# A fused top-k attention and gated feed-forward kernel: the second product's place in the order of TensorE

## The chip, the cores and the metric

The kernel runs on one core of a Trainium2 chip. A core has five engines that run their own queues in order and wait for each other by semaphores: TensorE (PE; its weight loads are shown apart as PEld), VectorE (DVE), ScalarE (ACT), GpSimd (POOL) and SyncE (SP, which here only issues DMAs). The metric is the time of one execution on the device in microseconds, given as the median over runs. Lower is better.

## The reference

Eight batches of eight heads, 576 tokens, head dimension 64. Each row of scores keeps its 32 largest entries, the rest is masked, and softmax and the product with V follow. The heads are then laid side by side, and a feed-forward part with a cosine gate is applied to the 4608 tokens. All in float32.

```python
scores = scale * np.matmul(q, k.transpose(0, 1, 3, 2))
kth = np.partition(scores, -top_k, axis=-1)[..., -top_k:-top_k + 1]
scores = np.where(scores >= kth, scores, -1000000000.0)
attn = softmax(scores)                       # sum in the denominator + 1e-09
x = np.matmul(attn, v)  ->  (B*S, H*D) = (4608, 512)
h = x @ w_in                                 # 512 x 2048
g = h * np.cos(h)
out = g @ w_out                              # 2048 x 512
```

## The kernel before, in words

**Units and slots.** The work of attention is cut into 144 units: 36 blocks of 128 tokens, each with four pairs of heads. A main loop has one slot a unit. In slot i, VectorE searches the 32 largest scores of unit i (four rounds of L359 and L364 on `rest`, then on `low`). Meanwhile ScalarE masks and exponentiates unit i-1 (L378, L387) and copies the scores of unit i+1 out of PSUM (`take_scores`, L253 and L257). GpSimd prepares unit i-2 for its transposition by DMA (`split`, L410 for the probabilities and L412 for the reciprocals `rden`), and it computes the lower halves of unit i's folded scores (L283, L292).

**TensorE's order** is written out by the emission of a slot, since each engine runs its instructions in the order in which they are emitted. A slot has three places where pieces of the feed-forward part are fed to TensorE. Feed A comes first. Then come the scores (L242) of the next units, two units in every even slot, and in slots with remainder 2 mod 4 the product P@V (`values`, L475) of the last block's four units. Feed B comes after the last round of the search has been emitted, and feed C closes the slot. So one block corresponds to four slots with remainders 0 to 3, and P@V of one block stands in each slot of remainder 2. After it VectorE multiplies with the reciprocals and writes the block's `xT` (`take_values`, L491 and L499), between the last two searches of that slot.

**The feed-forward part.** A block has eight items of the first product (`ff1`, L553). Each item computes two of the 16 column tiles of `h`, and the profile shows it as 16 matmul rows of 128 columns. Two items fill one PSUM bank. ScalarE empties a bank with two instructions (`take_first`, L567 and L569), into the scaled `g` and the rounded `x`. Two banks make one g tile of 1024 columns, so a block has two g tiles. A g tile then goes through GpSimd (`reduce_first`, L589; `reduce_second`, L598), ScalarE (`sines`, L608, in odd slots) and GpSimd again (`gate`, L615, which multiplies by the cosine). The block has also eight items of the second product (`ff2`, L628), two f each (f = 0, 2, ... 14), which read the gated g as weights and accumulate in one bank `o`; each is shown as four rows of 512 columns. Items f = 0 to 6 read the first g tile, f = 8 to 14 the second. ScalarE empties `o` (`take_second`, L638) and issues the DMA of the output. First and second product share two PSUM banks (tag `mm`).

**The planner.** `plan[i % 4]` lists for each feed of a slot what is tried there: 0 stands for an item of the first product, 1 for one of the second. An item is issued only if `can_first` or `can_second` allows it; otherwise it is passed over. `ff["tick"]` counts feeds, `ff["now"]` counts slots from 1. `can_second` asks that the slot count has reached a start value, that the w_out rows are decoded, and that the g tile in question was gated at least `lag` ticks ago. Gating is emitted in a slot just before feed B (`gate(1)`), and notes the tick of that slot's feed A. Sines are emitted in odd slots only, so a g tile is gated in an odd slot. `take_banks` empties full banks at several places of a slot. After the 144 slots a tail (`drain`, `forward`) works off what is left.

**The first slots.** The weights come as 64-bit words and are decoded in the first dozen slots by ScalarE, VectorE (L151) and GpSimd (L160). In slots 8 to 10 the fold is done by VectorE alone (`fold_now`, L275).

Of the kernel before, what the change touches and what calls it, by code (L numbers as in the profile page):

```python
# [30 lines left out]
def kernel(  # L31
# [16 lines left out]
    NP = H // 2  # L48
# [47 lines left out]
    ff = {"live": 0, "tick": 0, "now": 0, "end": False, "kind": 0, "half": 0, "open": 0, "late": False}  # L96
# [81 lines left out]
    NU = len(units)  # L178
# [333 lines left out]
    for w in widths:  # L512
# [10 lines left out]
    second = deque(  # L523
        (blk, i, f) for blk in blocks for i in range(blk["w"] // P) for f in range(0, NF, 2)
    )
# [125 lines left out]
        return ff["now"] > NP + 2 and (i % 4 > 0 or ff["live"] + staged() < CHUNKS)  # L651

    def can_second():
        if not second or ff["now"] < 2 * NP + 3:
            return False
        blk, i, f = second[0]

        lag = 3 if ff["now"] < NU - NP else 2
        gated = sum(ff["tick"] >= t + lag for t in blk["gated"])
        return gated * 1024 // blk["w"] >= f + 2 and wq["ready"] >= NC * NF // FC + f + 2  # L660

    def item(kind):
        if not (can_first, can_second)[kind]():
            return False
        if kind == 0:
            ff1(*first.popleft())
        else:
            ff2(*second.popleft())
        return True
# [68 lines left out]
    def send(x):  # L738
# [6 lines left out]

    plan = (
        ((0, 0), (1,), (1,)),
        ((0, 0), (1, 1), (0,)),
        ((0,), (1,), ()),
        ((1, 0, 0), (1, 1), ()),  # L750
    )

# [148 lines left out]
```

## Time and profile before

| | us |
|---|---|
| median of 3 runs | 1412.53 |
| lowest and highest | 1411.86, 1413.45 |
| span of the profiled execution, first to last instruction | 1410.6 |
| TensorE matmul rows busy | 1354.6 (96%) |
| VectorE busy | 1336.9 (95%) |
| ScalarE busy | 1140.9 (81%) |
| GpSimd busy | 1165.3 (83%) |

The profile is of one execution; it gives its span, and no time of its own beside it. A row of the order of time reads: start in us from the span's start, duration in us, engine, line, operation, output and inputs by tile name, shapes, and the number of instructions merged into the row; in brackets the idle time of the engine before it and what ended it. In the windows view the columns are the stretch, its length, the busy time of each engine with the number of instructions, the granted share of TensorE's clock, the DMA share and GB/s. Matmul rows overlap their successors a little, since their ends are modelled; the time that a piece takes is read from start to start.

The granted clock of TensorE is 0.975 as a mean over the span, and 1.00 in every stretch of 40 us between 120 and 1400 us. The first 120 us are different from the rest: TensorE is busy there for 68.3 of 120 us, and VectorE for 110.6.

### The profile page before, as it was taken

The page shows a single profiled execution, that of the slowest core. Times are in us where ns is not written, and L with a number is a line of the kernel's source. Part 1 is how long each engine was busy: PE and PEld are TensorE (multiplying, and loading weights), DVE is VectorE, ACT ScalarE, POOL GpSimd, SP SyncE. Part 2 cuts the span into 40 slices and gives each one's busy share as a digit, 9 for nine tenths or more (in the row PEclk, how much of TensorE's full clock was granted, in tenths as well). Part 3 has the DMA queues.
Part 4 walks back from the last instruction along what each step waited for, and adds up shares of the span by engine and source line. Part 5 has one row for each costly group of instructions (what it writes and reads, how often), then busy time and mean ns, then how long its engine had stood idle before and what let it go on. Part 6 is the DMA issues. An engine that isn't in the chain of part 4 may idle for free.

```text
span 1410.6 us, 32284 instructions
## 1 busy us (share of the span) xinstructions
PE 1354.6 (96%) x11264; PEld 977.2 (69%) x11264; DVE 1336.9 (95%) x5004; ACT 1140.9 (81%) x2043; POOL 1165.3 (83%) x804
## 2 busy tenths in 40 slices
PE   5558999999999999999999999999999999999998
PEld 3445777777777777777777777777777777777775
DVE  7999999999999999999999999999999999999931
ACT  7887888888888888888888888888888888888831
POOL 4778988888888888888888888888888888898810
PEclk6788999999999999999999999999999999999999
DMA  9566776867675576668666576666766566655540
GB/s 291 193 196 181 204 178 169 203 172 196 162 177 152 161 199 159 181 160 197 174 170 159 152 181 187 170 170 160 207 165 165 158 174 166 148 157 146 152 101 15
DMA packets 427442, 240.12 MB, mean 170 GB/s; under 512 B 375952, under 2 KB 392592, under 8 KB 427280
## 3 DMA queue, kind: packets, MB, share of 16 engines
q1 hardware_dynamic: 420720, 224.22, 61.3%
q10 hardware_dynamic: 6560, 13.85, 2.8%
q8 instruction: 88, 1.44, 0.4%
q14 instruction: 74, 0.61, 0.1%
HBM read 45.09 MB, written 101.19 MB: 104 GB/s over the span
## 4 chain that ended last, share of the span: by engine, by line
PE 91%; DVE 7%; ACT 1%; DMA 0%; POOL 0%; issue 0%; SPq 0%; POOLq 0%
PE o L628 36%; PE mm L553 35%; PE rim L475 10%; PE sc L242 8%; DVE top L359 3%; PE rim L242 2%; DVE rest L364 2%; DVE low L364 1%; DVE rest L267 1%; DVE w_out L151 0%; DVE w_in L151 0%; DMA st<-in_moe_w_in_dram 0%; PE warm L844 0%; DVE low L275 0%; ACT s L387 0%; ACT s L378 0%
## 5 line engine op out<-in xcount | busy, mean ns | idle before, releaser
L553 PEld LDWEIGHTS mm<-xT,w_in 128*128 128x128 f32 x4608 | 537.9, 192 | 70.4 <-issue 65.5
L553 PE MATMUL mm<-xT,w_in 128*128 128x128 f32 x4608 | 539.2, 275 | 2.4 <-DVE xT L491 1.7
L628 PE MATMUL o<-w_out,g 128*128 128x512 f32 x1152 | 524.7, 599 | 0.0
L359 DVE MAX8 top<-rest 128x8 f32<-128x288 f32 x1152 | 479.0, 451 | 0.0
L364 DVE MATCH_REPLACE8 rest<-top,rest 128x288 f32<-128x288 f32 x864 | 376.7, 444 | 0.0
L628 PEld LDWEIGHTS o<-w_out,g 128*128 128x128 f32 x1152 | 207.7, 190 | 219.5 <-issue 214.8
L410 POOL COPY halves<-s 128x2304 uint16<-128x2304 uint16 x140 | 294.9, 2107 | 43.3 <-ACT s L387 40.1
L378 ACT ACTIVATE s<-s,top 128x576 f32<-128x576 f32 x288 | 207.6, 768 | 111.1 <-DVE top L352 99.0
L359 DVE MAX8 top<-low 128x8 f32<-128x288 f32 x576 | 241.8, 449 | 0.4 <-POOL low L292 0.4
L387 ACT ACTIVATE s<-s,nd 128x576 f32<-128x576 f32 x288 | 220.4, 769 | 1.1
L292 POOL TENSOR_TENSOR low<-low,rest 128x576 int32<-128x576 int32 x141 | 199.3, 1413 | 11.0
L283 POOL TENSOR_TENSOR low<-s 128x576 int32<-128x576 int32 x141 | 199.6, 1415 | 6.4 <-ACT s L259 6.4
L598 POOL TENSOR_TENSOR x<-g,x 128x1024 f32<-128x1024 f32 x68 | 161.2, 2370 | 5.7
L242 PE MATMUL sc<-k,q 64*64 64x448 f32 (+1 forms) x1120 | 145.6, 564 | 16.2 <-DVE low L275 9.8
L615 POOL TENSOR_TENSOR g<-g,x 128x1024 f32<-128x1024 f32 x68 | 161.0, 2367 | 0.0
L257 ACT COPY s<-rim 64x256 f32<-64x256 f32 (+1 forms) x280 | 103.1, 368 | 61.6 <-PE rim L475 60.0
L475 PE MATMUL rim<-ring,v 128*64 128x128 f32 (+1 forms) x2560 | 139.0, 268 | 0.0
L475 PEld LDWEIGHTS rim<-ring,v 128*64 128x64 f32 x2560 | 130.0, 139 | 6.5 <-issue 5.7
L253 ACT COPY s<-sc 128x896 f32<-128x896 f32 (+1 forms) x144 | 128.4, 892 | 3.3 <-PE sc L242 3.2
L567 ACT ACTIVATE g<-mm 128x512 f32<-128x512 f32 x144 | 85.2, 592 | 56.5 <-PE mm L553 55.5
L364 DVE MATCH_REPLACE8 low<-top,low 128x288 f32<-128x288 f32 x288 | 125.4, 443 | 0.0
L267 DVE TENSOR_TENSOR rest<-sc,s 128x576 f32<-128x576 f32 x144 | 107.7, 748 | 7.1 <-ACT s L259 6.6
(55 smaller groups left out, 1155.7 us busy)
## 6 DMA issues: line engine op xcount, KB each, us to landing
rows<-halves SPq DMA_DIRECT2D x140, 640.0 KB, 3.5
out_dram<-ob ACTq DMA_DIRECT2D x36, 256.0 KB, 2.1
q<-in_q_dram SPq DMA_DIRECT2D x31, 288.0 KB, 4.4
st<-in_moe_w_in_dram SPq DMA_DIRECT2D x16, 512.0 KB, 5.8
v<-in_v_dram SPq DMA_DIRECT2D x32, 256.0 KB, 4.2
k<-in_k_dram SPq DMA_DIRECT2D x31, 144.0 KB, 4.2
k<-in_k_dram SPq DMA_DIRECT2D x32, 128.0 KB, 4.5
st<-in_moe_w_out_dram SPq DMA_DIRECT2D x8, 512.0 KB, 5.1
```

The costliest lines, as they stand in the source:

```text
L242: nc.tensor.matmul(to[r0 : r0 + rows, rim_bank(r0, j) if k0 else place(u["hp"], j), 0 : k1 - k0], st["q"][d, q0 : q0 + rows], st["k"][d, k ...
L283: nc.gpsimd.tensor_tensor(out=u["low"].bitcast(I32), in0=s[:, :, 0:HS], in1=s[:, :, HS:S], op=ALU.add)
L292: nc.gpsimd.tensor_tensor(out=low, in0=low, in1=u["rest"][:, :, HS:S].bitcast(I32), op=ALU.subtract)
L359: nc.vector.max(to[:, j], src[:, j])
L364: nc.vector.match_replace(rest[:, j], to[:, j], src[:, j], NEG)
L378: nc.scalar.activation(out=s[:, j], in_=s[:, j], func=AF.Prelu, bias=less[:, j], scale=1.0, alpha=FAR)
L387: nc.scalar.activation(out=s[:, j], in_=s[:, j], func=AF.Exp, bias=nd[:, j : j + 1], scale=SCALE, accum_out=den[:, j, 0:1],)
L410: nc.gpsimd.tensor_copy(out=halves[:, :, 0 : 2 * S], in_=s.rearrange("p (k h) -> p h k", h=2))
L475: nc.tensor.matmul(to[d, r], lhsT, rhs, start=(bank, j) not in begun, stop=c == NT - 1 and u in us[-2:] and r0 + rows == P,)
L553: nc.tensor.matmul(mm[:, at : at + w], w_in[f // FC][:, c, (f % FC) * P : (f % FC + 1) * P], blk["xT"][:, c], start=c == 0, stop=c == NC - 1,)
L598: nc.gpsimd.tensor_tensor(out=x, in0=g, in1=x, op=ALU.subtract)
L628: nc.tensor.matmul(o, g[:, at : at + P], w_out[f], start=f == 0, stop=f == NF - 1)
```

## The change

Two places of the planner are edited. The table for slots with remainder 1 and 2 gets another order: in remainder 1, feed B tries two items of the first product in place of two of the second, and feed C one of the second in place of one of the first; in remainder 2, feed A tries one of the second in place of one of the first. In `can_second`, the start value goes from 2*NP + 3 (11) to 2*NP + 2 (10), that is, from slot 10 to slot 9, and the lag from three ticks to one, except for the last four slots and the tail, where it stays at two. Nothing else is edited: all tiles, all instructions and their shapes are as before.

```diff
     def can_second():
-        if not second or ff["now"] < 2 * NP + 3:
+        if not second or ff["now"] < 2 * NP + 2:
             return False
         blk, i, f = second[0]
 
-        lag = 3 if ff["now"] < NU - NP else 2
+        lag = 1 if ff["now"] < NU - NP else 2
         gated = sum(ff["tick"] >= t + lag for t in blk["gated"])
...
     plan = (
         ((0, 0), (1,), (1,)),
-        ((0, 0), (1, 1), (0,)),
-        ((0,), (1,), ()),
+        ((0, 0), (0, 0), (1,)),
+        ((1,), (1,), ()),
         ((1, 0, 0), (1, 1), ()),
     )
```

## The prediction

> **What bounds the kernel now.** I read the page's busy shares and its chain first, then the busy time of each engine over single blocks, then the order of time on TensorE and on the engines that feed it.
>
> ```profile
> span 1410.6 us, 32284 instructions
> PE 1354.6 (96%) x11264; PEld 977.2 (69%) x11264; DVE 1336.9 (95%) x5004; ACT 1140.9 (81%) x2043; POOL 1165.3 (83%) x804
> PE 91%; DVE 7%; ACT 1%; DMA 0%; POOL 0%; issue 0%; SPq 0%; POOLq 0%
> ```
>
> ```profile
> core 0: us, PE busy (x) PEld busy (x) DVE busy (x) ACT busy (x) POOL busy (x), PEclk, DMA share, GB/s
> 707.87:744.57 36.70, 36.70 (x307) 26.50 (x305) 36.53 (x139) 30.82 (x55) 32.37 (x23) 1.00 0.69 174
> 110.50:116.00 5.50, 4.96 (x52) 3.72 (x53) 5.50 (x22) 3.83 (x8) 5.42 (x4) 0.50 0.21 53
> 121.00:132.00 11.00, 10.35 (x62) 7.37 (x61) 10.54 (x39) 10.25 (x17) 8.62 (x7) 1.00 0.98 233
> ```
>
> The first window is one block of 128 tokens (four slots), from the end of one P@V to the end of the next. TensorE is busy in all 36.70 us, VectorE in 36.53. TensorE has no hole at all, and the chain is 91% TensorE. So the steady state is TensorE's time, with VectorE 0.2 us behind: a hole opened in TensorE's order is added to the end. I number a block's slots by their remainder mod 4 and write F for an item of the first product (L553, 16 matmul rows), S for one of the second (L628, 4 rows), V for P@V (L475). One block on TensorE, in order of time:
>
> ```profile
> 704.22 3.71 PE L475 MATMUL rim<-ring,v 128*64 128x128 f32 x64
> 707.87 3.70 PE L628 MATMUL o<-w_out,g 128*128 128x512 f32 x8
> 711.40 3.73 PE L553 MATMUL mm<-xT,w_in 128*128 128x128 f32 x32
> 714.98 3.60 PE L628 MATMUL o<-w_out,g 128*128 128x512 f32 x8
> 718.41 3.73 PE L553 MATMUL mm<-xT,w_in 128*128 128x128 f32 x32
> 722.08 0.98 PE L242 MATMUL sc<-k,q 64*64 64x448 f32 x8
> ...
> 724.18 3.70 PE L628 MATMUL o<-w_out,g 128*128 128x512 f32 x8
> 727.71 3.73 PE L553 MATMUL mm<-xT,w_in 128*128 128x128 f32 x32
> 731.28 3.60 PE L628 MATMUL o<-w_out,g 128*128 128x512 f32 x8
> 734.72 3.73 PE L553 MATMUL mm<-xT,w_in 128*128 128x128 f32 x32
> ```
>
> Slot 2 ends with V at 707.87; then S0 S2, F0 F1 of the next block, S4 S6, F2 F3, scores, S8 S10, F4 F5, S12 S14, F6 F7, scores, V. (S0 is the item with f=0; S8 is the first that reads the second g tile.)
>
> **The change part by part.** Following the plan's counters through the loop, the new order from V is S4 S6, F F, S8 S10, F2 F3, scores, S12 S14, F4 F5 F6 F7, S0 S2, scores, V. Matmul count and shapes are the same; S14 and F4 trade places and every S comes two items (one 3.5 us piece) earlier. No DMA, POOL, VectorE or SP instruction is added.
>
> Order alone. A pair of S takes 3.43 to 3.53 us, a pair of F 3.57, or 3.67 ahead of scores (718.41 to 722.08). Scores now follow S instead of F, and one change S to F falls away: 0 to 0.1 us a block. I take -1 us in all (0 to -3).
>
> S0 S2 move to the end of slot 1. They need the gate of the first g tile and a bank. Rows of slot 1 and the start of slot 2:
>
> ```profile
> 731.48 0.60 ACT L567 ACTIVATE g<-mm 128x512 f32<-128x512 f32 x1 [0.73 <-PE mm L553]
> 737.06 0.60 ACT L638 ACTIVATE ob<-o 128x512 f32<-128x512 f32 x1
> 738.20 1.44 ACT L378 ACTIVATE s<-s,top 128x576 f32<-128x576 f32 x2 [0.54 <-POOL halves L412]
> ```
> ```profile
> 732.15 2.36 POOL L615 TENSOR_TENSOR g<-g,x 128x1024 f32<-128x1024 f32 x1
> 737.71 0.40 POOL L412 COPY halves<-rden 128x256 uint16<-128x256 uint16 x1
> ```
>
> That gate ends at 734.51 and S0 would come after four F at about 734.8: no wait, by 0.2 us. F6 F7 need the bank that the old o leaves; S14 now ends at 727.71, and its copy (0.60 us, L638) can run where ScalarE waits 0.73 us ahead of L567, so done by about 731.4, when F6 wants it. Both are close and cost 0 here; if the cover fails, some tenths of a us a block.
>
> S8 S10 move from slot 0 to slot 3, and this is the part that costs. They need the gate of the second g tile, which runs in slot 3:
>
> ```profile
> 710.43 0.40 POOL L412 COPY halves<-rden 128x256 uint16<-128x256 uint16 x1 [0.61 <-DVE rden L400]
> ...
> 712.29 1.42 POOL L292 TENSOR_TENSOR low<-low,rest 128x576 int32<-128x576 int32 x1
> 713.66 2.38 POOL L615 TENSOR_TENSOR g<-g,x 128x1024 f32<-128x1024 f32 x1
> ```
> ```profile
> 708.76 0.76 DVE L491 TENSOR_TENSOR xT<-rim,ring 128x256 f32<-128x256 f32 x2 [0.17 <-ACT s L257]
> ...
> 710.22 0.15 DVE L400 RECIPROCAL rden<-den 128x2 f32<-128x2 f32 x1
> ```
>
> The gate ends at 716.04; TensorE stands at S8's place at 714.98. Before, S4 S6 stood there and S8 came at 724.18, 8 us after the gate. Can the gate move forward? Its queue is full from L412 on (between the rows shown runs L283), L412 waits for the reciprocal, that for xT, and xT waits for V (through ScalarE's L257). All of it hangs on V's end: 8.1 us from V to the gate's end against 7.1 us of S S F F. If TensorE gets later, so does V, and the chain with it; the hole does not close by a shift of phase. The first and the last of the 31 blocks in which this holds (S8 in slots 15, 19, ... 135):
>
> ```profile
> 198.79 2.38 POOL L615 TENSOR_TENSOR g<-g,x 128x1024 f32<-128x1024 f32 x1
> 1302.05 2.37 POOL L615 TENSOR_TENSOR g<-g,x 128x1024 f32<-128x1024 f32 x1
> ```
> ```profile
> 200.04 3.60 PE L628 MATMUL o<-w_out,g 128*128 128x512 f32 x8
> 1303.30 3.60 PE L628 MATMUL o<-w_out,g 128*128 128x512 f32 x8
> 714.87 0.30 PEld L628 LDWEIGHTS o<-w_out,g 128*128 128x128 f32 x2
> ```
>
> 201.17 - 200.04 = 1.13, 716.04 - 714.98 = 1.06, 1304.42 - 1303.30 = 1.12; the others lie between 0.98 and 1.13, mean 1.06. Two small terms come on top: what waits is the weight load, 0.11 us ahead of the matmul (714.87), and a release from POOL takes about 0.09 us (L412 ends at 738.11, ScalarE starts at 738.20). So 1.26 us a block, and 31 x 1.26 = 39 us (34 at 1.1, 46 at 1.5). What is queued behind S8 is all of TensorE: S10, F2 F3, scores, V.
>
> The end. From slot 139 on the lag is 2, so there S8 S10 are passed over, and by slot 142 the order is the old one; the tail is unchanged. On the way F6 F7 of slot 141 find o still open and must take F4 F5's bank: two copies like L567, about 1.3 us, plus release: +1.5 once (0 to 2).
>
> The start. The first S may now go in slot 9, ahead of scores and V of slot 10:
>
> ```profile
> 107.57 0.70 PE L242 MATMUL rim<-k,q 64*64 64x128 f32 x8 [5.70 <-ACT s L257]
> 111.04 1.77 PE L242 MATMUL sc<-k,q 64*64 64x448 f32 x8 [2.76 <-DVE low L275]
> ...
> 118.62 3.70 PE L628 MATMUL o<-w_out,g 128*128 128x512 f32 x8
> ...
> 129.98 1.27 PE L553 MATMUL mm<-xT,w_in 128*128 128x128 f32 x9 [0.65 <-ACT x L569]
> ```
> ```profile
> 108.75 2.35 POOL L615 TENSOR_TENSOR g<-g,x 128x1024 f32<-128x1024 f32 x1
> 130.19 2.38 POOL L615 TENSOR_TENSOR g<-g,x 128x1024 f32<-128x1024 f32 x1
> ```
>
> S0 waits for the gate until 111.1, the moment at which scores went before, so the holes ahead of it aren't filled. At the 0.50 clock of that window S0 S2 take some 5 to 6 us, and V ends about 4.5 us later (123). In slot 11 the gate hangs on V as above: 132.57 + 4.5 = 137. TensorE is at S8 by 123 + 7.1 = 130 and waits 7 us, a hole like those of slot 10, so likely with slow matmuls behind it (+2). F2 F3 of slot 12 then start at about 142 instead of 130, with two S more done (3.5): +8 us (+3 to +11).
>
> Sum: 39 + 8 + 1.5 - 1 = 47.5 us. The profiled span is 1410.6, the median 1412.53, so 1.9 us lie around the span or between executions, and I leave them as they are: 1412.5 + 47.5 = 1460.
>
> A hole of 1.26 us could also cost clock. The trace: after holes of 5.70 and 2.76 us the granted clock was 0.50 (110.50 to 116), while around the hole at 129.98 it stayed 1.00 (121 to 132). The Trainium skill, "TensorE: Matmul & The Clock Gate", section "A second HAM failure mode: psum-queue depth-cycling", says that short idle times between matmul groups, if frequent, can make the clock swing between half and full. That speaks against this change and is the third rival below; this trace, with one short hole and no loss, does not bear it out.
>
> **The rivals.**
> 1. The hole closes: S8 finds its gate done. It is faster then: no 39, no 8, S0 S2 fall in the idle time of slots 9 and 10 (-3.5), and the order saves 1 to 3: about 1407. It decides where the gate ends 6.9 us after V or sooner, 1.2 us earlier than in any of the 31 blocks; for that L412 would have to stop waiting for the reciprocal (0.61 us) and more. 4%.
> 2. The thin covers in slot 1 fail too. If F6 had to wait for F4 F5's bank, as in slot 141, it is 1.4 us more a block: 1460 + 43 = 1503. Against it: at 734.72 F6 took the bank that was read at 731.48, not o's, read only at 737.06, so the bank that is free longest is taken, and that is now o's. If only the gate of S0 is late, 0.1 to 0.4 us a block: 1463 to 1472, within the range. 5% for the large one.
> 3. The clock falls at each hole. By the 110.50 window half speed lasts up to 5 us, 2.5 us a block: 31 x 2.5 = 78, so 1538. 3%.
>
> **How the numbers follow.** My forecast has 88%: 1460, a hole in every block. Its own bounds: 34 + 3 - 3 + 0 gives 1447; 46 + 11 + 2 + thin covers gives 1474. Rivals 1 to 3 lie outside with 12% together, so 1446 to 1475 holds 8 in 10. A measurement tells about 0.2% (2.8 us) from no change. Faster: 4% (rival 1). Within 0.2%: 2%, out of the forecast's own low edge if half of the holes vanish and the order saves more. Slower: 94%.
>
> **What would show it.** In the changed profile a block should last about 37.9 us, TensorE should wait about 1.3 us at L628 with POOL's L615 as what ended it, once a block, 31 times and once for some 7 us near 130; VectorE's wait at xT should grow by about 1.2 us; the granted clock should stay 1.00. Waits at L553 for ScalarE's L638 or L569 in slot 1 would be rival 2. If the block still lasts 36.7 us, the chain from V to the gate was shorter than I read it, and the prediction is wrong.

## The result, and the profile after

The changed kernel takes 1463.43 us (median; 1462.49 to 1464.52) against 1412.19 us for the kernel before, measured beside it: a ratio of 1.0359, with a 95% interval from 1.0344 to 1.0374. It is slower by 51.2 us, where 47.5 were forecast.

The page of the changed kernel, the lines that answer to those of before:

```profile
span 1462.0 us, 32212 instructions
PE 1365.9 (93%) x11264; PEld 975.4 (67%) x11264; DVE 1343.4 (92%) x5004; ACT 1140.5 (78%) x2043; POOL 1164.3 (80%) x804
PE 72%; POOL 11%; DVE 9%; ACT 3%; issue 3%; DMA 1%; SPq 0%; POOLq 0%; ACTq 0%
```

The chain is the line to read. TensorE's share of it fell from 91% to 72%, and GpSimd, which had no share before, now holds 11%. The work of GpSimd is the same as before (1164.3 us busy against 1165.3); it has become something that TensorE waits for. The list of waits says where. The first row is of TensorE, the other three of VectorE; each gives the total in us, the number of waits and the longest:

```profile
PE o L628 <- POOL g L615: 49.2, 33, 13.5
DVE rest L267 <- ACT s L257: 21.8, 34, 0.7
DVE den L395 <- ACT s L387: 15.0, 34, 5.6
DVE xT L491 <- ACT s L257: 12.8, 26, 1.0
```

There are 33 waits of L628 for the gate: 31 of them at S8 of slots 15 to 135, one at S0 of slot 9 and one at S8 of slot 11. The windows view shows one block, and the short stretch behind the hole of slot 11. Of the three numbers at the end of a row the first is the granted clock:

```profile
core 0: us, PE busy (x) PEld busy (x) DVE busy (x) ACT busy (x) POOL busy (x), PEclk, DMA share, GB/s
701.16:739.14 37.98, 36.97 (x307) 26.43 (x305) 36.72 (x141) 30.81 (x55) 32.32 (x23) 1.00 0.62 171
136.90:143.31 6.41, 6.35 (x8) 2.71 (x9) 6.36 (x25) 1.30 (x3) 5.16 (x5) 0.55 0.49 167
```

A block went from 36.70 to 37.98 us at a full clock, and TensorE, which had no idle time in a block, now has about one us. In order of time on TensorE, from the end of P@V on:

```profile
739.14 3.70 PE L628 MATMUL o<-w_out,g 128*128 128x512 f32 x8
742.68 3.73 PE L553 MATMUL mm<-xT,w_in 128*128 128x128 f32 x32
747.35 3.70 PE L628 MATMUL o<-w_out,g 128*128 128x512 f32 x8 [0.94 <-POOL g L615]
750.88 3.73 PE L553 MATMUL mm<-xT,w_in 128*128 128x128 f32 x32
...
760.18 7.31 PE L553 MATMUL mm<-xT,w_in 128*128 128x128 f32 x64
767.33 3.60 PE L628 MATMUL o<-w_out,g 128*128 128x512 f32 x8
```

and on VectorE (first row) and GpSimd over the same time:

```profile
740.03 0.76 DVE L491 TENSOR_TENSOR xT<-rim,ring 128x256 f32<-128x256 f32 x2 [0.43 <-ACT s L257]
```
```profile
741.71 0.40 POOL L412 COPY halves<-rden 128x256 uint16<-128x256 uint16 x1 [0.64 <-DVE rden L400]
...
744.92 2.37 POOL L615 TENSOR_TENSOR g<-g,x 128x1024 f32<-128x1024 f32 x1
```

The pair F F ahead of S8 takes 4.67 us from start to start in place of 3.57: a hole of 1.10. S8 starts at 747.35, 0.06 us after the gate's end at 747.29. The gate ends 8.15 us after P@V, as it did before (8.17 for the block quoted in the prediction): the chain xT, reciprocal, L412, folds, gate kept its length, and TensorE arrives before it. All 31 blocks are alike:

```profile
215.66 1.55 PE L628 MATMUL o<-w_out,g 128*128 128x512 f32 x3 [1.00 <-POOL g L615]
1317.01 3.70 PE L628 MATMUL o<-w_out,g 128*128 128x512 f32 x8 [0.94 <-POOL g L615]
```

These are S8 of slots 19 and 135, 29 blocks apart: 37.98 us a block. The same place before (S S at 200.04 and 1303.30, slots 19 and 139, 30 blocks) gives 36.78. The difference is 1.20 us a block, 37.3 us over 31 blocks. The hole itself is 1.10 of it; the other 0.10 is the pair S8 S10 behind it, which takes 3.53 us (747.35 to 750.88) where the S S pair at this place before took 3.43 (714.98 to 718.41).

The rest lies at the start and near the end. TensorE's rows at both places:

```profile
111.05 5.82 PE L628 MATMUL o<-w_out,g 128*128 128x512 f32 x8 [13.46 <-POOL g L615]
...
122.98 3.70 PE L628 MATMUL o<-w_out,g 128*128 128x512 f32 x8
...
136.96 6.51 PE L628 MATMUL o<-w_out,g 128*128 128x512 f32 x8 [6.70 <-POOL g L615]
143.31 3.73 PE L553 MATMUL mm<-xT,w_in 128*128 128x128 f32 x32
```
```profile
1350.24 3.73 PE L553 MATMUL mm<-xT,w_in 128*128 128x128 f32 x32
1355.99 3.84 PE L553 MATMUL mm<-xT,w_in 128*128 128x128 f32 x32 [2.02 <-ACT x L569]
...
1365.40 3.73 PE L553 MATMUL mm<-xT,w_in 128*128 128x128 f32 x32
1370.90 3.84 PE L553 MATMUL mm<-xT,w_in 128*128 128x128 f32 x32 [1.77 <-ACT x L569]
```

F2 F3 of slot 12 start at 143.31 in place of 129.98, with two S more done (3.5): 9.8 us lost. At slots 139 and 141 a pair of F takes 5.75 and 5.50 us in place of 3.57, since it must take the bank of the pair before it: 2.2 and 1.9. Together 37.3 + 9.8 + 4.1 = 51.2, which is the whole difference.

### The profile page after: what moved, and what is told of

Same layout as the page of the kernel before. It is cut to its first block, busy times and chain, and to the rows that moved or that the text cites. A ratio compares the mean times of both kernels' runs of the same rounds, so it can differ in the third digit from the quotient of the medians.

```text
span 1462.0 us, 32212 instructions
## 1 busy us (share of the span) xinstructions
PE 1365.9 (93%) x11264; PEld 975.4 (67%) x11264; DVE 1343.4 (92%) x5004; ACT 1140.5 (78%) x2043; POOL 1164.3 (80%) x804
## 4 chain that ended last, share of the span: by engine, by line
PE 72%; POOL 11%; DVE 9%; ACT 3%; issue 3%; DMA 1%; SPq 0%; POOLq 0%; ACTq 0%
PE o L628 27%; PE mm L553 26%; PE rim L475 10%; PE sc L242 7%; POOL g L615 5%; DVE top L359 4%; POOL low L292 3%; PE rim L242 2%; ACT s L257 2%; DVE rest L364 1%; DVE xT L491 1%; DMA st<-in_moe_w_in_dram 1%; POOL low L283 1%; POOL halves L412 1%; DVE low L364 1%
## 5 line engine op out<-in xcount | busy, mean ns | idle before, releaser
L628 PE MATMUL o<-w_out,g 128*128 128x512 f32 x1152 | 533.0, 606 | 49.2 <-POOL g L615 49.2
L628 PEld LDWEIGHTS o<-w_out,g 128*128 128x128 f32 x1152 | 209.3, 191 | 277.9 <-issue 222.2
L387 ACT ACTIVATE s<-s,nd 128x576 f32<-128x576 f32 x288 | 220.7, 769 | 2.5 <-ACT ob L638 0.4
L257 ACT COPY s<-rim 64x256 f32<-64x256 f32 (+1 forms) x280 | 102.9, 368 | 95.2 <-PE rim L475 93.6
L267 DVE TENSOR_TENSOR rest<-sc,s 128x576 f32<-128x576 f32 x144 | 108.0, 750 | 28.4 <-ACT s L257 21.8
L589 POOL TENSOR_SCALAR x<-x 128x1024 f32<-128x1024 int32 x68 | 71.2, 1046 | 69.5 <-ACT x L569 69.5
```

The source lines that it names most:

```text
L387: nc.scalar.activation(out=s[:, j], in_=s[:, j], func=AF.Exp, bias=nd[:, j : j + 1], scale=SCALE, accum_out=den[:, j, 0:1],)
L628: nc.tensor.matmul(o, g[:, at : at + P], w_out[f], start=f == 0, stop=f == NF - 1)
```

## The experiments

Two explanations are put against each other. Theory G: S8 waits for a gate that hangs on P@V through VectorE and GpSimd. The rival, theory O: the new order itself costs, by the mix of matmuls or the use of the two banks. Each run is compared with the kernel before, measured beside it (1412 us).

**The gate earlier.** In slots of remainder 3 the sine and the gate are emitted ahead of the fold. In the 31 blocks this changes the order of GpSimd alone.

```diff
         ff["late"] = False
+        if i % NP == 3:
+            sines(1)
+            gate(1)
         topk_first(u, w)
...
-        if i % 2:
+        if i % NP == 1:
             sines(1)
...
-        gate(1)
+        if i % NP != 3:
+            gate(1)
```

> The changed kernel, but in slots of remainder 3 the sine and the gate are emitted ahead of the fold, so that GpSimd runs the gate ahead of L283 and L292 and not behind them. TensorE's order is that of the changed kernel. Theory G (the hole is S8 waiting for a gate that hangs on V through the reciprocal, L412, L283 and L292): the gate ends some 2.8 us earlier after V, ahead of S8's place, the holes at L628 go in all 31 blocks and most of the 7 us hole of slot 11, a block lasts about 36.7 us, the time is 1414 to 1424. Theory O (the new order of the matmuls or the use of the two banks costs): the time stays at 1460 or more. In both, the low half comes to VectorE 2.4 us later, which it has just room for; if not, VectorE waits at L359 for L292.

1423.95 us, 1.0085 times the kernel before (1.0069 to 1.0100). GpSimd's order after a P@V that ends at 718.80, and TensorE's:

```profile
721.36 0.40 POOL L412 COPY halves<-rden 128x256 uint16<-128x256 uint16 x1 [0.59 <-DVE rden L400]
722.20 2.36 POOL L615 TENSOR_TENSOR g<-g,x 128x1024 f32<-128x1024 f32 x1 [0.44 <-DVE rest L267]
```
```profile
718.80 3.70 PE L628 MATMUL o<-w_out,g 128*128 128x512 f32 x8
722.34 3.73 PE L553 MATMUL mm<-xT,w_in 128*128 128x128 f32 x32
725.91 3.60 PE L628 MATMUL o<-w_out,g 128*128 128x512 f32 x8
...
738.64 7.54 PE L553 MATMUL mm<-xT,w_in 128*128 128x128 f32 x64
746.02 3.60 PE L628 MATMUL o<-w_out,g 128*128 128x512 f32 x8
```

The gate ends 5.8 us after P@V, S8 comes 7.1 us after it and waits for nothing. Of the 51.2 us, 39.5 are gone. Some 30 of them go in the 31 blocks, where TensorE's order is that of the changed kernel: from the end of P@V in slot 14 to that in slot 138 they take 1147.4 us (37.01 a block) in place of 1177.2 (37.98). That speaks for G and against O. Six more go ahead of slot 14, and four at the end; there the order does change, since a gate that is emitted earlier counts more ticks, so that S8 S10 are no longer passed over in slot 139 and the two bank holes do not arise. What is left in a block: the four F take 7.38 us, where the changed kernel took 7.15.

**The other tile.** The same without touching GpSimd's order: the wait is taken away by taking away what is waited for. This kernel leaves out the second half of the gated values.

```diff
         for f in range(f0, f0 + 2):
-            g = blk["g"][f // per]
+            g = blk["g"][0]
```

> The changed kernel, but all eight items of the second product read the first g tile of the block, so that S8 to S14 no longer depend on the second gate. Left out: the second half of the gated values takes no part in the product. All instructions stay, in the same order and of the same shapes. Theory G: no hole at L628 in the steady state nor in slot 11, about 36.7 us a block, 1463 less 31 x 1.2 less 8 to 10 at the start: 1416 to 1420. Theory O: stays at 1460 or more.

1428.17 us (ratio 1.0117, 1.0101 to 1.0132): the holes of the 31 blocks are gone here too, but the time is 8 us above the expected range. The main reason is that the four F took 7.37 us here as well (31 x 0.23 = 7), so that a block lasts 37.01 us and not 36.7. The rest is about 1 us less gained at the start than the 8 to 10 expected (slot 14 comes 7.3 us earlier than in the changed kernel), and 1 us more lost at the end: the bank holes of slots 139 and 141 were in the expectation, but behind the one at slot 139 (2.01 us idle, at 1318.82) the pair of F ran at a slower clock and took 5.39 us in place of 3.77.

**The gate longer**, in the changed kernel and in the kernel before.

```diff
             eng = nc.vector if ff["end"] else nc.gpsimd
+            if not ff["end"] and len(blk["gated"]) == 1:
+                nc.gpsimd.tensor_scalar(out=x, in0=x, scalar1=1.0, scalar2=0.0, op0=ALU.mult, op1=ALU.add)
```

> The changed kernel with one more GpSimd instruction of about 1.05 us (L589's form) ahead of the second gate of each block; it multiplies the cosine by 1. Theory G: the chain from V to S8 is longer by its whole length in every block: 32 x 1.05 = 34, so 1497. Theory O: GpSimd is 80% busy and not the bound, no change (1463).

> The kernel before with the same extra GpSimd instruction ahead of the second gate of each block. Theory G: S8 stands 8 us behind that gate there, so the second gate has slack: 1412, within 2 us. If the kernel before already hung on GpSimd's chain: +34 as in the changed one.

Before: 1412.56 us (1.0004, 0.9994 to 1.0014), so nothing, as expected: there S8 stands 8 us behind the gate. In the changed kernel: 1548.4 us (1.0966, 1.0949 to 1.0982), 85 us more and not 34. The 1.05 us of theory G are there, but not alone. TensorE, and the window of the slow stretch:

```profile
702.76 3.73 PE L553 MATMUL mm<-xT,w_in 128*128 128x128 f32 x32
708.50 5.40 PE L630 MATMUL o<-w_out,g 128*128 128x512 f32 x8 [2.00 <-POOL g L617]
713.73 3.73 PE L553 MATMUL mm<-xT,w_in 128*128 128x128 f32 x32
```
```profile
708.50:712.00 3.50, 3.50 (x6) 1.56 (x7) 3.50 (x16) 1.60 (x4) 3.34 (x3) 0.67 0.66 127
422.97:426.50 3.53, 3.53 (x5) 1.53 (x6) 3.53 (x16) 1.63 (x4) 3.38 (x3) 0.52 0.60 143
```

Behind the longer hole the pair S8 S10 takes 5.23 us in place of 3.54, with a granted clock of 0.67 and 0.52 in its first 3.5 us. So in 28 of the 31 blocks a hole that grew by 1.05 us costs 1.7 us more in clock. Half of that instruction's width was the test between the two.

```diff
-                nc.gpsimd.tensor_scalar(out=x, in0=x, scalar1=1.0, scalar2=0.0, op0=ALU.mult, op1=ALU.add)
+                nc.gpsimd.tensor_scalar(out=x[:, 0:512], in0=x[:, 0:512], scalar1=1.0, scalar2=0.0, op0=ALU.mult, op1=ALU.add)
```

> The changed kernel with an extra GpSimd instruction of half the width ahead of the second gate of each block (about 0.55 us). Theory G: the hole at S8 grows from 1.2 to about 1.75 us a block: 32 x 0.55 = 18, so 1481, if the clock stays at 1.00. If a hole of this length already lets the clock fall as in the run with the longer gate, 1.7 us more in most blocks: up to 1535.

1487.15 us (1.0528, 1.0512 to 1.0544), 24 us above the changed kernel, 0.7 a block, with no loss of clock:

```profile
1024.67 3.73 PE L553 MATMUL mm<-xT,w_in 128*128 128x128 f32 x32
1029.97 3.70 PE L630 MATMUL o<-w_out,g 128*128 128x512 f32 x8 [1.57 <-POOL g L617]
1033.51 3.73 PE L553 MATMUL mm<-xT,w_in 128*128 128x128 f32 x32
```
```profile
1029.97:1033.50 3.53, 3.53 (x8) 1.63 (x9) 3.53 (x15) 1.67 (x4) 2.94 (x3) 1.00 0.87 153
```

The hole is 5.30 - 3.57 = 1.73 us and S8 S10 take their 3.54. The extra instruction lasts 0.61 us and not the 0.55 expected (L616 at 1026.86), and the hole grew by 0.63. The chain's length goes into the time one for one, as G says.

**One part of the change alone.** Start value and lag with the old plan:

```diff
-        if not second or ff["now"] < 2 * NP + 3:
+        if not second or ff["now"] < 2 * NP + 2:
...
-        lag = 3 if ff["now"] < NU - NP else 2
+        lag = 1 if ff["now"] < NU - NP else 2
```

> Start value and lag of the change, with the old plan. By the plan's counters S0 S2 then come right behind F4 F5 in slot 1, S8 S10 in slot 3 as in the changed kernel. Theory G: the hole at S8 stays (1.2 us), and a second one opens at S0, about 2 to 3 us ahead of the gate of the first tile; with a hole above 2 us the clock falls as in the run with the longer gate (1.7 us more). A block lasts 39 to 43 us, the time is 1500 to 1610. If it were the new plan that costs and not the lag (theory O): near 1412.

1615.89 us (1.1446, 1.1431 to 1.1462), 6 us above the expected range. Both holes are there, the one at S0 (3.09 us idle), behind which the clock fell in 20 of 32 blocks (6.60 us for a pair of S, in the row below), and the one at S8 as in the changed kernel. In the other 12 blocks the pair behind S0's hole kept its speed, 3.54 us at 1058.39:

```profile
1006.66 3.73 PE L553 MATMUL mm<-xT,w_in 128*128 128x128 f32 x32
1013.48 6.77 PE L628 MATMUL o<-w_out,g 128*128 128x512 f32 x8 [3.09 <-POOL g L615]
1020.08 3.73 PE L553 MATMUL mm<-xT,w_in 128*128 128x128 f32 x32
...
1038.72 3.70 PE L628 MATMUL o<-w_out,g 128*128 128x512 f32 x8 [0.95 <-POOL g L615]
```

The new plan with the old lag and start value (the rest of the diff undone):

> The new plan with the old start value and lag. By the plan's counters S8 comes in slot 0 again, 8 us behind its gate, but o stays open until slot 2, so that F6 F7 must take F4 F5's bank in every block, as in slot 141 of the changed kernel. Theory G: no hole at L628; a hole at L553 for ScalarE's L569 of about 1.9 us a block, 33 x 1.9 = 63, so about 1475 (up to 1530 if the clock falls too). If the plan alone were harmless: 1412.

1467.62 us (1.0392, 1.0378 to 1.0406). No hole at S8, one at F6 in each block, 1.42 us long (4.99 less 3.57) where 1.9 were expected, and the F behind it keep their speed (3.68 us to the next S). A block lasts 38.32 us, 1.55 more than before, which makes 48 of the 56 us; most of the rest is lost ahead of slot 14 (5.7):

```profile
1025.06 3.73 PE L553 MATMUL mm<-xT,w_in 128*128 128x128 f32 x32
1030.05 3.84 PE L553 MATMUL mm<-xT,w_in 128*128 128x128 f32 x32 [1.26 <-ACT x L569]
```

So each half of the change is slow by a wait of its own: the lag alone by two gates, the plan alone by a bank. Together the bank and the gate of S0 are free, and the gate of S8 is left.

**What is left after the early gate.** Two runs, one on top of the other: the copy of the old o ahead of ScalarE's mask in slots of remainder 1, then also the old start, with two missing S caught up in slot 12.

```diff
         if i % NP == 1:
             sines(1)
+        if i % NP == 1 and full and full[0][0] == take_second:
+            take, *what = full.popleft()
+            take(*what)
         if w:
             mask(w)
```

> The run with the early gate, and in slots of remainder 1 the copy of the old o (L638) goes ahead of ScalarE's mask, so that its bank is free sooner. If the 0.24 us that each block still has above 36.70 is F6 waiting for that copy, the four F of slot 1 take 7.14 us and not 7.38, a block lasts 36.70 and the time is 1424 - 31 x 0.24 = 1416.5. If it is something else, 1424.

1415.3 us (1.0022, 1.0013 to 1.0032). The four F are back at 7.15 us (734.47 to 741.62):

```profile
734.47 7.31 PE L553 MATMUL mm<-xT,w_in 128*128 128x128 f32 x64
741.62 3.60 PE L628 MATMUL o<-w_out,g 128*128 128x512 f32 x8
```

```diff
+    special = {10: ((), (1,), ()), 12: ((0, 0), (1, 1), (1, 1))}
...
-        if not second or ff["now"] < 2 * NP + 2:
+        if not second or ff["now"] < 2 * NP + 3:
```

> The same, and the start of the kernel before: the first S in slot 10 behind V, none ahead of scores and V, and the two S that are missing caught up in slot 12. If what is left above the kernel before is the start (holes and slow matmuls around 111 us), the time is that of the kernel before, 1411 to 1414; if the new order itself costs or gains, it lies apart from 1412 by that.

(`special` replaces the plan in slots 10 and 12.) 1411.93 us, ratio 1.0001 (0.9993 to 1.0010): the time of the kernel before, with the order of the changed kernel in every block from slot 13 on. The blocks show it more sharply than the whole: from the end of P@V in slot 14 to that in slot 138, 31 blocks take 1140.04 us here (159.24 to 1299.28), and 1139.95 in the kernel before (156.24 to 1296.19). So the order of the matmuls, once its waits are gone, costs nothing in a block that can be measured, and gains nothing. This closes rival O.

**A gain at the start?** The kernel before with one sine in slot 8, so that S0 S2 run in TensorE's idle time of slot 9:

```diff
+        if i == 2 * NP:
+            sines(1)
         ff["late"] = True
         gate(1)
```

> The kernel before, with the start value 2*NP + 2 and one sine emitted in slot 8, so that the first g tile is gated in slot 8 and S0 S2 run in slot 9, where TensorE is idle; lag 3 and the old plan put S8 back into slot 0 afterwards. The steady state is that of the kernel before. Two items (3.5 us) move into idle time: 1408 to 1410. If the idle time there is not TensorE's to use (V or the fold gets later): 1412 or more.

1413.57 us (1.0012, 1.0003 to 1.0021), no gain. S0 S2 did run at 100.89, but then slot 11 had no S to feed, and TensorE stood there:

```profile
100.89 5.40 PE L628 MATMUL o<-w_out,g 128*128 128x512 f32 x8 [3.24 <-POOL g L615]
...
129.47 5.32 PE L553 MATMUL mm<-xT,w_in 128*128 128x128 f32 x32 [4.09 <-ACT x L569]
```

The idle time was moved from slot 9 to slot 11, where the F behind it ran at 5.3 us for the slower clock.

## Why the prediction was right

Its steps one by one.

- *The hole at S8.* Forecast 1.26 us a block and 39 in all, measured 1.20 and 37.3. That the two lie so close is in part luck. Of the two small terms added to the 1.06 (0.11 for the weight load, 0.09 for the release) little came: S8 starts 0.06 us after the gate's end, not 0.20. In their place came the 0.10 us by which S8 S10 take longer behind a hole, which the prediction did not have. The rows quoted as the first and the last of the 31 blocks (200.04 and 1303.30) are those of slots 19 and 139; at slot 15 of the kernel before the gate ended 1.84 us behind S8's place and not 0.98 to 1.13, but the changed kernel has a hole like the others there (0.95 us idle). The argument that the hole does not close by a shift of phase is what the 31 equal holes, the early gate and the two longer gates bear out: the time follows the length of the chain from P@V to the gate.
- *The start.* S0 at 111.05 (111.1 forecast), end of P@V at 122.98 (123), S8 at 136.96 (137), F2 F3 at 143.31 (142), slow matmuls in both places. 9.8 us for 8.
- *The end.* Slot 141 cost 1.9 (1.5 forecast). The prediction left out the same hole between slots 139 and 140: with S8 S10 passed over, F2 F3 follow F0 F1 at once while o is open, 2.2 us. That is the largest missing term.
- *The order alone.* Taken at -1 us, it is 0 (0.1 us over 31 blocks, in the run that also has the old start): what scores save by following S instead of F (S S ahead of scores 3.53 (767.33 to the scores at 770.86), F F ahead of scores 3.67), the pairs behind the removed change lose again (3.57 + 3.53 against 3.44 + 3.67).
- *The thin covers of slot 1.* They held in the changed kernel (four F in 7.15), though only because TensorE comes 1.2 us late: with the hole closed the copy of o was late by 0.23 us a block. "Some tenths of a us" was the right size.
- *VectorE's wait at xT.* It was to grow by 1.2 us and did not: 0.43 us in the block shown, 12.8 us in all against 7.1. VectorE has the idle time, but ScalarE gives it earlier in the block: ScalarE's copies wait for F F, which are late, and VectorE then waits at L267 for L257 (21.8 us in all, 34 times) and at L395 for L387. TensorE's terms alone add up to the whole difference, so nothing is left for it in the time.
- *The rivals.* Rival 1 (the hole closes) was put 1.2 us of chain away. Moving the gate by 2.4 us closed the hole; no run shows how much less would have done. The time was then 1424 and not rival 1's 1407, since the start and the copy of o still cost. Rival 2's bank hole came in every block only with the plan alone. Rival 3, the clock, did not come: 1.00 in the blocks. It was nearer than its 3% said, since one more us of GpSimd work brought it in 28 of 31 blocks, at 1.7 us a block and not the 2.5 that the rival reckoned with.

## What to carry to other kernels

Before an item is moved forward on a saturated engine, work out the earliest end of its input from the event that both hang on (here the end of P@V: 8.1 us to the gate, 7.1 us to the item). If the input's chain hangs on the engine itself, being late does not close the hole, and its length is paid in every round. A lag counted in places of a program is no time: the old lag and plan left S8 8 us of slack behind its gate, the new ones none.

## What the runs showed of the hardware

Short holes on TensorE cost no clock up to a point, and then more than themselves. Holes of 0.94 us (the changed kernel) and of 1.57 to 1.72 us idle (the half-width run), once a block of some 38 us, left the clock at 1.00. Holes of 2.00 to 2.14 us brought it down in 28 of 31 blocks of the longer gate, with 0.67 and 0.52 in the first 3.5 us after the two shown, and 1.7 us lost in such a block. The length alone does not decide: three blocks of that run were spared, and at slot 139 a hole of 2.02 us in the changed kernel (1355.99) was followed by a pair of F at full speed (3.77 us), while one of 2.01 us in the run with the other tile was followed by a slow pair (5.39).

The traces show what decides. Behind 120 us every half-clock stretch begins on a grid of 3.41 us, and in the longer gate's blocks it lasts one step of it. Four steps of this grid in that run, around the hole that ends at 708.50 and around a spared one, which ends at 790.01:

```profile
706.29:709.70 3.41, 1.41 (x5) 0.69 (x5) 3.41 (x14) 3.37 (x8) 3.41 (x2) 1.00 1.04 189
709.70:713.11 3.41, 3.41 (x5) 1.33 (x4) 3.41 (x15) 1.52 (x4) 3.17 (x4) 0.50 0.55 190
784.79:788.20 3.41, 3.15 (x29) 2.96 (x27) 3.41 (x15) 3.38 (x7) 3.25 (x4) 1.00 0.71 240
788.20:791.61 3.41, 1.60 (x4) 0.87 (x5) 3.41 (x14) 3.02 (x7) 3.41 (x2) 1.00 0.92 192
```

The first hole lies whole in one step, in which matmul rows are busy for 1.41 us (41%), and the next step has half the clock. The second hole lies across two steps, with 3.15 and 1.60 us busy (92% and 47%), and its pair of S keeps its speed (3.53 us, 790.01 to 793.54). Counted over the steps of all twelve traces from 120 us to near the end (some 4,500), all 57 full-clock steps that were busy for 42% or less were followed by one at half clock, and none of those busy for 43% or more was. The busy time is that of rows with modelled ends, and in the first 120 us a step of 47% was followed by half clock too, so the border is one of these dense stretches. The Trainium skill, "TensorE: Matmul & The Clock Gate", section "HAM oscillation — how this bites in real kernels", gives idle gaps above some 3.4 us as the limit; here gaps of 2.0 us were enough where one step held them, so the measurement decides for this kernel.
